# DeltaNet and maxout on one core: the first chunk's inverse by doubling on TensorE, and pairs of chunks shifted by one

## The chip, the cores and the metric

The kernel runs on one core of a Trainium2 chip. The metric is the device time of one execution, in microseconds (us). All profiles quoted are in the fast state. Each run of a changed kernel stood beside runs of the kernel before on the same chip. A ratio is the mean time of one kernel's fast runs over the mean of the other's of the same rounds, so it isn't quite the ratio of the medians that are quoted. A span is the length of the one profiled execution.

Engines: PE is TensorE, DVE is VectorE, ACT is ScalarE, POOL is GpSimd, SP is SyncE, which here only issues transfers.

## The reference

```python
# q, k, v: (4, 8, 768, 48), beta: (4, 8, 768), all float32
k_n = k / (norm(k) + 1e-6)
for t in range(S):
    y[:, :, t] = q[:, :, t] @ state
    v_old = k_n[:, :, t] @ state
    state = state + beta[t] * outer(k_n[:, :, t], v[:, :, t] - v_old)
x = y.transpose(0, 2, 1, 3).reshape(3072, 384)
h = maximum(maximum(x @ w1, x @ w2), x @ w3)      # three 384 x 768 matrices
return h @ w_out                                   # 768 x 384
```

The recurrence is computed in 12 chunks of 64 steps. Within a chunk it needs the inverse of a unit triangular 64x64 matrix for each batch and head. Between chunks only a state is handed on.

## The kernel before

Two chunks make a group of 512 tokens; there are six groups. For each chunk TensorE forms Gram products of the keys (`p_g`). Two chunks at a time, VectorE inverts the four 32x32 diagonal blocks of each head by forward substitution, 31 steps of two operations, with one matrix on each of 128 partitions:

```python
def solve(m):                      # m: pair of chunks (2m, 2m+1)
    ...                            # norms and beta: ten small operations
    for j in range(BL - 1):        # BL = 32
        nc.vector.tensor_tensor(out=t_v, in0=x[:, j, ...], in1=y[:, 0:a, j, ...], op=ALU.mult)
        nc.vector.tensor_tensor(out=y[...], in0=y[...], in1=t_v, op=ALU.subtract)
        yield                      # another part of the program is placed here
    ...                            # to DRAM as y_d and x_d, back as ut2, t1 and ut: SP's queue
```

TensorE then joins the blocks (`p_z`, `p_j`), takes the state into account (`p_k`, `p_q`), solves (`p_u`), moves the state on (`p_s`), forms the output (`p_y`) and transposes it (`p_x`) into `xt`. These are the *small products*: a chunk's `p_u`, for instance, has 64 of 64x48. The maxout part of a group follows:

```python
def ffn(m):
    for f in range(6):
        for i in range(3):                       # a maxout step: p_h
            ...                                  # three products, 128 x 128 by 512 columns
            # i == 0: ACT copies p_h to h; else DVE takes max(h, p_h)
    for i in range(4):
        ...                                      # p_o: six products of 384 columns
```

The weights come as 24 pieces, each fetched into one of four buffers (`w_bits`) and converted by three operations on VectorE (`mant`), two on GpSimd (`mant`, `w_sb`) and one on ScalarE (`up`). All transfers that matter are issued in order on SP's queue: fetches of pieces, loads of keys and queries, and the solve's results. The opening is in program order. Behind it a scheduler orders each engine's instructions by its own estimate of when they are ready; that order is fixed when the program is built.

The solve of a group's pair of chunks runs about one group ahead of its use:

```python
for m in range(GROUPS):
    for i, _ in enumerate(ffn(m)):
        ...
        if i == SOLVE:                  # 12 of 22 steps
            solving = solve(m + 2)      # z of that group: step 3 of the next group
        if i >= SOLVE:
            some(solving, 4)
        links(m + 1, LINKS.get(i, ""))  # small products of the next group, spread
```

## Time and profile before

| | before |
|---|---|
| median of 4 runs (lowest, highest) | 621.76 us (621.56, 623.07) |
| span of the profiled run | 622.2 us |
| TensorE busy, idle | 544.3, 77.9 us |
| VectorE busy | 317.6 us |
| first maxout product | 74.4 us |
| second half of group 0 starts | 143.8 us |

The prediction shows the strips, the stretches by group and the chain. Three more stretches will be compared later. Each line has: stretch, length, busy time (and instructions) of PE, of its weight loads, of DVE, ACT and POOL, then the granted PE clock, the DMA share and GB/s.

```profile
0.00:74.40 74.40, 34.65 (x743) 27.79 (x743) 41.63 (x109) 26.68 (x44) 23.60 (x49) 0.66 0.77 156
74.40:143.80 69.40, 48.49 (x962) 38.67 (x963) 57.78 (x143) 17.34 (x34) 23.72 (x27) 0.92 0.43 102
...
143.80:622.20 478.40, 461.18 (x6014) 258.49 (x6014) 218.16 (x498) 109.47 (x177) 39.97 (x47) 0.99 0.31 62
```

At 143.8 us half of group 0's maxout products are done: in this kernel these are the first three of the six blocks `f`, of both chunks (the `p_x` of chunk 1 came at 98.0 us).

### The profile page before, as it was taken

What the parts mean: (1) busy time and instruction counts of PE and PEld (TensorE: products, weight loads), DVE (VectorE), ACT (ScalarE), POOL (GpSimd) and SP (SyncE); (2) the same over time, 40 slices, a digit from 0 to 9 for tenths busy, and PEclk for the clock granted to TensorE, in tenths of its full rate; (3) what the DMA queues carried; (4) which work ended last, traced back from release to release, by engine and by line L of the source; (5) the groups of instructions that cost most, each with busy time, mean ns of one, the idle gap of its engine ahead of it and who ended that gap; (6) DMA issues with size and microseconds to landing.
All of it is one profiled execution on the core that took longest, in us unless ns stands there. A gap on an engine that the chain in (4) does not pass through costs nothing.

```text
span 622.2 us, 17590 instructions
## 1 busy us (share of the span) xinstructions
PE 544.3 (87%) x7718; PEld 324.9 (52%) x7718; DVE 317.6 (51%) x748; ACT 153.5 (25%) x255; POOL 87.3 (14%) x123
## 2 busy tenths in 40 slices
PE   5361786676799999999999999999999999999997
PEld 4251675452555554655655545555555555554444
DVE  0797159998364982369722499132596222101110
ACT  4333222323421232221332121432112120110001
POOL 7102204445141002000110000200000100000000
PEclk9656599887799999999999999999999999999999
DMA  9775813553771544352355321542103400020002
GB/s 196 141 162 123 184 34 110 137 112 72 205 124 20 108 99 91 79 95 52 77 111 98 65 52 27 106 91 44 36 1 79 77 2 3 3 49 1 0 0 51
DMA packets 158412, 48.47 MB, mean 78 GB/s; under 512 B 143296, under 2 KB 153344, under 8 KB 158336
## 3 DMA queue, kind: packets, MB, share of 16 engines
q1 hardware_dynamic: 156096, 46.87, 36.3%
q8 instruction: 60, 0.98, 0.7%
q10 hardware_dynamic: 2112, 0.39, 0.4%
q14 instruction: 16, 0.13, 0.1%
q0 software_dynamic: 128, 0.10, 0.1%
HBM read 31.56 MB, written 15.73 MB: 76 GB/s over the span
## 4 chain that ended last, share of the span: by engine, by line
PE 66%; DVE 23%; issue 4%; ACT 2%; DMA 2%; POOL 1%; SPq 0%; POOLq 0%; ACTq 0%; DVEq 0%
PE p_h L591 39%; PE p_o L615 11%; DVE tmp L376 7%; DVE y_bl L382 7%; PE p_t L285 3%; PE p_g L307 3%; PE p_u L516 2%; PE p_s L534 2%; PE p_k L488 2%; PE p_y L551 1%; PE p_q L488 1%; PE p_z L447 1%; DVE h L601 1%; PE p_j L466 1%; DVE mant L208 1%
## 5 line engine op out<-in xcount | busy, mean ns | idle before, releaser
L591 PE MATMUL p_h<-xt,w_sb 128*128 128x512 f32 (+1 forms) x702 | 301.4, 578 | 18.8 <-POOL w_sb L216 7.2
L591 PEld LDWEIGHTS p_h<-xt,w_sb 128*128 128x128 f32 x702 | 131.3, 195 | 145.6 <-issue 117.2
L601 DVE TENSOR_TENSOR h<-h,p_h 128x512 f32<-128x512 f32 (+1 forms) x78 | 50.2, 644 | 148.5 <-PE p_h L591 147.3
L615 PE MATMUL p_o<-wo_sb,h 128*128 128x384 f32 x288 | 96.5, 489 | 1.6 <-DVE h L601 1.5
L615 PEld LDWEIGHTS p_o<-wo_sb,h 128*128 128x128 f32 x288 | 53.6, 190 | 39.7 <-DVE h L601 4.6
L376 DVE TENSOR_TENSOR tmp<-x_bl,y_bl 128x31 f32<-128x31 f32 (+15 forms) x186 | 69.2, 372 | 4.9
L382 DVE TENSOR_TENSOR y_bl<-y_bl,tmp 128x31 f32<-128x31 f32 (+15 forms) x186 | 65.8, 354 | 4.6
L599 ACT COPY h<-p_h 128x512 f32<-128x512 f32 (+1 forms) x39 | 21.6, 553 | 129.7 <-PE p_h L591 129.7
L258 POOL TENSOR_TENSOR v_t<-v_t,nrm 128x768 f32<-128x768 f32 x12 | 17.8, 1482 | 175.1 <-DMA v_t<-in_v_dram 51.1
L307 PE MATMUL p_g<-kqt 64*64 64x64 f32 (+1 forms) x1280 | 33.4, 250 | 8.4 <-ACT kqt L291 7.1
L307 PEld LDWEIGHTS p_g<-kqt 64*64 64x64 f32 x1280 | 28.3, 149 | 16.8 <-ACT kqt L291 10.0
L291 ACT COPY kqt<-p_t 128x1024 f32<-128x1024 f32 (+1 forms) x28 | 24.6, 890 | 28.6 <-PE p_t L285 28.5
L285 PE MATMUL p_t<-ident,kpad 128*128 128x128 f32 x96 | 19.1, 333 | 11.5 <-DMA kpad<-in_k_dram 11.5
L623 ACT COPY o_sb<-p_o 128x384 f32<-128x384 f32 x24 | 11.5, 479 | 67.6 <-PE p_o L615 64.5
L203 POOL TENSOR_SCALAR mant<-mant 128x384 f32<-128x384 f32 x24 | 14.4, 600 | 82.7 <-DVE mant L199 57.7
L540 DVE TENSOR_TENSOR st<-st,p_s 128x768 f32<-128x768 f32 x11 | 10.5, 951 | 28.3 <-PE p_s L534 28.3
L456 POOL COPY ut<-ut 32x512 f32<-32x512 f32 x24 | 14.6, 608 | 72.9 <-DMA ut<-y_d 71.9
L285 PE MATMUL p_t<-ident,qpad 128*128 128x128 f32 x96 | 17.7, 313 | 7.1 <-DMA qpad<-in_q_dram 5.2
L447 PE MATMUL p_z<-ut,at 64*32 64x32 f32 x768 | 10.8, 203 | 14.8 <-DMA ut<-y_d 14.8
L317 DVE TENSOR_TENSOR pt<-p_g,mask 128x512 f32<-128x512 f32 x24 | 16.4, 687 | 11.2 <-PE p_g L307 11.1
L216 POOL TENSOR_TENSOR w_sb<-mant,up 128x384 int32<-128x384 int32 x18 | 18.8, 1045 | 23.9 <-DVE mant L212 12.7
L325 ACT COPY at<-p_g 128x512 f32<-128x512 f32 x24 | 14.0, 585 | 32.1 <-DVE pt L317 26.6
(74 smaller groups left out, 444.6 us busy)
## 6 DMA issues: line engine op xcount, KB each, us to landing
w_bits<-in_moe_w_dram SPq DMA_DIRECT2D x18, 384.0 KB, 4.3
at_d<-at SPq DMA_DIRECT2D x48, 128.0 KB, 3.2
qpad<-in_q_dram SPq DMA_DIRECT2D x48, 96.0 KB, 3.4
v_t<-in_v_dram SPq DMA_DIRECT2D x24, 192.0 KB, 4.3
out_dram<-o_sb SPq DMA_DIRECT2D x48, 96.0 KB, 2.2
kpad<-in_k_dram SPq DMA_DIRECT2D x44, 96.0 KB, 3.1
x_bl<-at_d SPq DMA_DIRECT2D x24, 128.0 KB, 3.1
y_d<-y_bl SPq DMA_DIRECT2D x12, 256.0 KB, 3.5
```

The source lines that it names most:

```text
L216: nc.gpsimd.tensor_tensor(out=dst.bitcast(I32), in0=mant_v.bitcast(I32), in1=up_v, op=ALU.add)
L258: nc.gpsimd.tensor_tensor(out=vts[c], in0=vts[c], in1=nrm[:, :, :, None].to_broadcast([128, 2, H, D]), op=ALU.mult,)
L285: nc.tensor.transpose(p_t[:, i, j * 128 : (j + 1) * 128], src[:, 2 * j : 2 * j + 2], ident,)
L291: nc.scalar.copy(kqt.rearrange("p j b i t -> p i (j b) t")[:, some], p_t.rearrange("p i (x t) -> p i x t", t=C)[:, some],)
L307: nc.tensor.matmul(p_g[rows(bb ^ (g * i)), par, c0 : c0 + C * (1 + whole)], kq[:, 0], kq if whole else kq[:, i],)
L376: nc.vector.tensor_tensor(out=t_v, in0=x[:, j, None, j + 1 :].to_broadcast([128, a, b]), in1=y[:, 0:a, j, None].to_broadcast([128, a, b]), ...
L382: nc.vector.tensor_tensor(out=y[:, 0:a, j + 1 :], in0=y[:, 0:a, j + 1 :], in1=t_v, op=ALU.subtract,)
L488: nc.tensor.matmul(p_b[rows(bb), par, c0 : c0 + D], kqt[g][rows(par), j, bb ^ g, i], st[rows(par), bb ^ g, g, j],)
L591: nc.tensor.matmul(p_h, w_sb[i][:, t, f * 128 : (f + 1) * 128], xt[:, t, lo : lo + w], start=(t == 0), stop=(t == KT - 1),)
L599: nc.scalar.copy(h, p_h)
L601: nc.vector.tensor_tensor(out=h, in0=h, in1=p_h, op=ALU.max)
L615: nc.tensor.matmul(p_o, hs[f][:, i * 128 : (i + 1) * 128], wo_sb[:, f], start=(f == 0), stop=(f == FT - 1),)
```

## The change

The intent is to start maxout long before the first solve on VectorE could be finished. Chunk 0 is solved on TensorE by doubling: blocks of 1, 2, 4 ... 32 are combined in six levels of small products. The forward substitution takes the other chunks in pairs shifted by one, (1,2), (3,4) ... (11). Groups 0 and 1 go through maxout in halves of 256 columns, one chunk each, so that chunk 0 need not wait for chunk 1. The core of the diff, with cuts:

```diff
+    class First:                                  # chunk 0
+        def step(self, lv, part):                 # one of six levels, half of the heads
+            ...  # p_a: 16 products of 64x64 (not in the last level)
+            ...  # p_r: 16 products of 64x112 (64x48 in the last two)
+            ...  # DVE masks p_a into zt, ACT copies p_r into ar
...
-    early = FT // 2 if m == 0 else 0              # only half of group 0's p_h in halves
-    for lo in (0, TOK // 2):
-        for f in range(early):
-            yield from hidden(f, lo, TOK // 2)
+    parts = 2 if m < 2 else 1
+    w = TOK // parts
+    for i in range(parts):
+        for f in range(FT):
+            yield from hidden(f, i * w, w)
+        for j in range(4 // parts):
+            yield from result(i * (4 // parts) + j)
...
-            nc.vector.tensor_scalar(               # a weight piece
-                out=mant_v, in0=high, scalar1=0x7FFFFFFF, scalar2=None,
-                op0=ALU.bitwise_and,
-            )
+            nc.scalar.activation(
+                out=mant_v.bitcast(FP32), in_=high.bitcast(FP32),
+                func=mybir.ActivationFunctionType.Abs,
+            )                                      # and joined one piece later
...
-                solving = solve(m + 2)             # begun at step 12, used in the next group
+    for p in range(4, PAIRS + 1):                  # the pair of chunks (2p-1, 2p)
+        m = p - 2
+        at_end = 37 if m == 2 else 18
+        SOLVES[p] = ((m - 1, at_end), (m - 1, at_end + 2), (m, 7))
+        # plan of group m: z of that pair at step 10, chunk 2p-1 ready (x) at step 18
```

The Gram products of keys and queries, one product of 128 columns for half of the units before, are two of 64 columns now. The opening, up to the end of chunk 0, is in program order.

## The prediction

> **What bounds the kernel now.** I read the page's strips first, then the chain that ended last, then busy time by stretches, then single instructions.
>
> ```profile
> PE   5361786676799999999999999999999999999997
> DVE  0797159998364982369722499132596222101110
> PEclk9656599887799999999999999999999999999999
> ```
>
> Each character is 15.6 us. TensorE (PE) is full from the twelfth slice to the end at full clock. The loss lies in the first eleven, where VectorE (DVE) has its nines. The chain says the same: PE carries 66%, DVE 23%.
>
> ```profile
> 0.00:74.00 74.00, 34.25 (x738) 27.48 (x742) 41.63 (x109) 26.53 (x44) 23.60 (x49) 0.66 0.77 155
> 74.00:223.00 149.00, 120.76 (x2126) 82.58 (x2119) 108.73 (x258) 41.41 (x77) 42.23 (x49) 0.92 0.48 108
> 302.00:391.00 89.00, 86.92 (x1291) 49.70 (x1289) 50.22 (x122) 24.32 (x37) 6.33 (x7) 1.00 0.37 73
> 391.00:478.00 87.00, 85.80 (x1288) 49.59 (x1288) 43.62 (x98) 20.79 (x32) 4.86 (x6) 1.00 0.26 54
> ```
>
> The columns are stretch, length, busy time of PE, weight loads, DVE, ACT and POOL, PE clock, DMA share, GB/s. The first stretch ends where maxout begins; in it the inverses of the first two chunks are solved on DVE. The second is the first group of maxout (149 us); the last two are ordinary groups (89 and 87 us) with PE over 97% busy. So about 74 + 60 us at the start are in play, nothing after.
>
> ```profile
> 556.14 46.35 PE p_h L591 x108
> 602.49 15.49 PE p_o L615 x48
> 228.77 3.00 DMA y_d<-y_bl
> 231.82 1.97 DMA ut<-y_d
> ```
>
> These chain lines (start, length, what) give the last group, maxout alone: 46.35 + 15.49 = 61.8 us. The lower two are the hand-over after a solve: 5.2 us from the last DVE operation to p_z.
>
> **What the Trainium skill says.** "FP8 and Floating Point Precision", TensorE Precision Notes, gives true FP32 four passes through the array. With the 2.4 GHz of "TensorE: Matmul & The Clock Gate", a 512-column product is an estimated 4 x 512 / 2.4 = 853 ns; the trace has 46.35 / 54 = 858 ns (two recorded instructions per product). So late PE time cannot shrink. "TensorEngine Tiling (Array Packing)", Key Properties, says tiles work independently. The trace agrees: 64 recorded 64x48 instructions of p_k add 1.08 us to the chain, 17 ns each, though one is listed at 220 ns. That makes the new inverse on PE cheap. "SBUF — State Buffer", "SBUF: two separate sides", calls the port that DVE and GpSimd share an exclusive lock. The trace agrees: the same 135-element operation takes 0.30 us alone and 1.09 us beside a weight addition of POOL.
>
> ```profile
> 31.15 0.30 DVE L376 TENSOR_TENSOR tmp<-x_bl,y_bl 128x135 f32<-128x135 f32 x1
> 101.51 1.09 DVE L376 TENSOR_TENSOR tmp<-x_bl,y_bl 128x135 f32<-128x135 f32 x1
> 101.30 1.14 POOL L216 TENSOR_TENSOR w_sb<-mant,up 128x384 int32<-128x384 int32 x1 [0.77 <-DVE mant L212]
> ```
>
> **The change, part by part.** The built program's order on each engine shows where things stand, without times.
>
> *The first chunk.* Before, maxout waits for the first solve (DVE 28.7 to 52.4 us, 31 steps of two operations), two DMA hops, p_z, p_j, p_u, p_y and p_x. Now chunk 0 needs keys, norms, one transposition and six doubling levels on PE. My sum: keys land at 6.3 us as before; 16 warm-up instructions and cold transpositions leave kqt at about 8.5; level masks (21 small DVE operations, 0.17 us each) delay the two norm sums (0.55 each) to 8; ten small DVE/ACT operations of 0.2 to 0.25 give the factors at 11.7; four 512-element key operations (0.65) end at 14.3. They hold two of three PSUM pairs, so other keys' products wait; transposed blocks are masked by about 18.5, and two units are turned by 19.5. A level is two halves, each with 32 recorded 64x64 instructions (17 ns: 0.54 us) and 32 of 64x112 (four passes in four tiles: 0.75 us). PE needs 2.6 us, ACT two copies of 896 (about 0.93 each, from 0.80 for 768), DVE four masks of 256 (0.41). With latency and inserted transpositions and weight pieces I take 3.3, 3.3, 4.2, 4.2, 3 and 2: 20 us. Then u, p_y, y, p_x, xt in halves, 4.5 us. Maxout starts at about 44 instead of 74.4 us.
>
> *The pairs shifted by one chunk.* Chunks (1,2), (3,4) ... (11) still make six solves. DVE loses no solve. Off its path come 24 `mant` operations of 0.51 us (12 us, now on ACT). It gains about 15 us of masks and keys in the opening.
>
> *Chunk by chunk.* The first half of group 0 (18 products of 256 columns, two outputs) can run while DVE solves (1,2). It waits for that solve and the weights. Before, a solve with 13 pieces filled DVE from 93.3 to about 146 us. Of those 53 us the new order removes 13 x 0.35 (at least) for `mant`, four masks (0.6), three maxima (0.33) and a subtraction (0.9), some 9, and adds three sums of norms (1.5) and the small prelude (about 2.2). So the solve lasts 46 to 48 us: 44 to 91. PE, needing some 34 us there, idles. Behind it DVE has seven pieces left; with the POOL operations (0.60 + 1.05 us) that is 12 to 14 us, since POOL sets the pace. The order puts both outputs before the next p_z: the last piece leaves another 4.5 us of p_o. Then p_z 0.7, z copies 1.3, p_j 1, ut 1.3, p_u 1.1, u 0.8, p_y 1.1, y 0.95, p_x 0.7, xt 0.8: 10 us. The second half starts at 91 + 13 + 4.5 + 10 = 118 us.
>
> *The rest at PE's rate.* Maxout left: 162 products of 256 columns at 0.435 us (18 recorded ones took 4.17 us, at most 0.46 per product with fill), 216 of 512 at 0.86, 22 outputs at 3.87: 70.5 + 185.8 + 85.1 = 341. Small work, counted from the order: ten p_k (1.08), p_q (0.93), p_u (1.08), p_y (1.0) and p_x (0.68), nine p_s (1.08), p_z and p_j (0.97), 28 groups of four transpositions (0.44), and 17 double gram products (1.0): 104. Gram products in pairs of 64 columns, instead of 128 at once, add 0.1 us per chunk, included. With 2.5% for bubbles (89 and 87 us against 61.8 + 23.4 = 85.2 of such work) it is 456. The solve hand-overs of (3,4) and (5,6) are nearly even with PE's work. For (3,4), DVE has a prelude of 3.5 us, 62 operations interleaved at about 0.32 (20), a copy 1, 22 maxima of 0.35 (7.7), four updates of 0.87 (3.5), six norm sums of 0.46 (2.8) and 3 of masks and norms: 41, plus 5 of hand-over. PE has until that p_z 23 steps of three products (30), two outputs (7.7) and some 10 of small work: 48. For (5,6) I count 42 + 5 against 44. I give 5 us for both. The last output's copy and DMA: 3 us.
>
> Sum: 118 + 456 + 5 + 3 = **582 us**, 6.4% shorter. Calibration on the kernel before: at 143.8 us it had an estimated 454 us of PE work and took 478, so 24 us of stalls. My 19 us after 118 (11 + 5 + 3) is lower because the order has room for DMA.
>
> **Rivals.**
> 1. *The new opening is slow.* A chain of PE, DVE and ACT with short bursts could run at half clock: "TensorE: Matmul & The Clock Gate", Part 1, says idleness returns the gate to half rate, and the trace shows 0.50 for 52 to 74 us, when PE was busy 9.3 of 22 us. PE is fuller in the new levels, which speaks against it. If it came, levels cost 5 to 6 us: maxout at 56, time 594.
> 2. *DVE and POOL simply become the bound in the first group.* Starting maxout 30 us earlier does not finish (1,2) 30 us earlier if pieces, locks and solve pile up; I have charged most of this. If each of the 24 pieces costs one full lock of 0.8 us extra, 12 to 15 us more: about 596. If instead moving Abs to ACT unties DVE from POOL, the hand-over shrinks by 10: about 570.
> 3. *Input transfers.* DMA was 77% busy to 74 us (155 GB/s). By 44 us the new opening wants about 7.6 MB (eight key and four query units of 192 KB, two v of 384, four products of 256, blocks 0.5 MB: 4.6; eight weight pieces of 384 KB: 3), 49 us at that rate. Weights are last, so pieces come late rather than keys; this could add 5 to 8 us, but the first half was waiting anyway.
> 4. *Hidden anyway.* If the solve of (3,4) took the place of the first, the early start would be lost: about 605. Against it, its 41 us lie beside 48 us of PE work.
>
> **Range and chances.** Rivals 1 and 2 each reach up by 12 to 15, the favourable side of 2 down by 12; PE's remaining work is known to some 6 us. So 564 to 602. Faster by over 2% means below 609.5 us, which needs both adverse rivals: 0.96 faster, 0.035 the same, 0.005 slower.
>
> **What would show it.** The first p_h at 40 to 48 us; levels about 20 us long at a clock near 0.9; the solve of (1,2) ending at 86 to 96 us with DVE over 90% busy; p_h after chunk 1's xt at 112 to 124; then PE over 96% busy to the end, ordinary groups still 85 to 89 us, the last group 62. It is wrong if maxout starts after 55 us, if PE has long gaps after 125 us, or if the group steps became longer.

## More of the kernel before

What PE waited for shows in the view of waits (what waited, for whom: us in total, times, longest).

```profile
PE p_z L447 <- DMA ut<-y_d: 14.8, 4, 8.5
...
PE p_h L591 <- DVE h L601: 5.4, 4, 2.5
```

The first product after a solve waits for its results (9.0 of the 14.8 us in the opening). PE waits for a maximum of VectorE only 5.4 us in all.

## The result, and the profile after

| | before | after |
|---|---|---|
| median (lowest, highest), 4 runs each | 621.76 (621.56, 623.07) | 648.38 (645.65, 650.37) us |
| ratio, 95% interval | | 1.0421 (1.0379 to 1.0462) |
| span of the profiled run | 622.2 | 648.4 us |
| TensorE busy, idle | 544.3, 77.9 | 571.7, 76.7 us |
| first maxout product | 74.4 | 55.3 us |
| second half of group 0 starts | 143.8 | 145.0 us |

The changed kernel is 4.2% slower. The prediction of 582 us was 66 us too low, far outside its range. The totals already say something odd: TensorE does 27.4 us more and idles just as long as before. The strips of the page after (16.2 us a character):

```profile
PE   6866787779797999796989988999899999999997
...
DVE  6357998435972379522398131695323963201110
...
PEclk7986687979998999899998989999999999999999
```

PE is better filled in the first four slices than before. But its sixes, sevens and eights go on to the middle of the kernel, where the strip before had only nines. The stretches, to set beside the three above:

```profile
0.00:55.30 55.30, 39.60 (x1147) 35.50 (x1147) 27.58 (x75) 24.40 (x43) 23.08 (x49) 0.82 0.81 151
55.30:145.00 89.70, 66.83 (x1019) 50.93 (x1019) 65.79 (x149) 39.60 (x79) 36.10 (x45) 0.83 0.58 133
...
145.00:648.40 503.40, 465.31 (x6569) 294.00 (x6568) 235.36 (x571) 106.15 (x178) 28.43 (x31) 0.98 0.28 54
```

Maxout starts 19 us sooner, but the first half and what follows it take 89.7 us, and at 145.0 us TensorE has 465.3 us of work left. The kernel before had 461.2 left at 143.8 us. So there is no lead left by then. (At both marks as much of `p_h` is left; the kernel before has two more of the 24 outputs to do.) Behind it after takes 25.0 us more: 4.1 of work and 20.9 of idle time (38.1 against 17.2). Half clock is in that work: where the view of windows has a granted clock of 0.50, TensorE is busy for 19.5 us of this stretch after and 12.0 before, which makes some 3.7 us of the difference. The chain's end is as it was: the lengths of the last group's two parts are the same to 0.01 us.

```profile
581.99 46.35 PE p_h L808 x108
628.34 15.49 PE p_o L825 x48
```

What PE waited for, after:

```profile
PE p_h L808 <- DVE h L818: 16.1, 10, 3.7
PE p_g L370 <- issue: 7.1, 5, 2.2
...
PE p_j L678 <- issue: 5.7, 4, 1.9
...
PE p_z L659 <- DMA ut<-y_d: 0.5, 1, 0.5
```

The waits for solves are nearly gone. In their place PE waits for maxima, and for nothing that the profile shows ("issue"). Adding up all such lines from 145.0 us on, I get 15.6 us of issue and 12.9 of maxima after; in the stretch from 143.8 us before they were 2.9 and 1.7. Three lines from the timeline of PE after show the first (start, length, instruction, in brackets the gap before it and what ended it):

```profile
296.61 1.09 PE L370 MATMUL p_g<-kqt 64*64 64x64 f32 x58 [1.60 <-issue]
...
301.44 0.37 PE L744 MATMUL p_s<-u,kpad 64*64 64x48 f32 x10 [0.89 <-issue]
...
305.71 0.39 PE L370 MATMUL p_g<-kqt 64*64 64x64 f32 x10 [2.18 <-issue]
```

From 290 to 306.7 us the small products of a chunk stand in one run, without a product of maxout between them. The gaps cut through groups (10 of 64 are left after the last one). In another such run, from 372 us, they come at multiples of 128 recorded products, each with its weight load. The second kind, on PE and then on DVE:

```profile
341.19 4.42 PE L808 MATMUL p_h<-xt,w_sb 128*128 128x512 f32 x6 [3.16 <-DVE h L818]
```

```profile
338.17 1.58 DVE L587 TENSOR_TENSOR tmp<-x_bl,y_bl 128x256 f32<-128x256 f32 x1
339.67 0.54 DVE L309 TENSOR_REDUCE ksum<-ksq 128x8 f32<-128x384 f32 x1
...
340.47 0.67 DVE L818 TENSOR_TENSOR h<-h,p_h 128x512 f32<-128x512 f32 x1
```

The maximum that PE waits for stands behind steps of a solve in VectorE's fixed order, one of them lengthened from 0.42 to 1.58 us beside a GpSimd operation at 337.9 us. After the gap six recorded products take 4.42 us instead of the 2.6 of the last group; from 342.3 to 345.7 us the granted clock is 0.50.

Between these there is the hand-over of the first solve. It ends on VectorE at 105.67 us. SP's queue, after:

```profile
115.56 0.33 SPq L232 DMA_DIRECT2D w_bits<-in_moe_w_out_dram  x1
115.99 1.15 SPq L601 DMA_DIRECT2D y_d<-y_bl  x2
```

The result leaves 10.3 us late, behind fetches of weight pieces that wait for a free buffer. The last piece is done at 125.8 us; only then can the first half's `p_o` end, and `p_z` comes at 127.4. PE, after:

```profile
125.87 1.56 PE L825 MATMUL p_o<-wo_sb,h 128*128 128x384 f32 x4 [0.43 <-POOL wo_sb L278]
127.36 1.16 PE L659 MATMUL p_z<-ut,at 64*32 64x32 f32 x68
```

### The profile page after: what moved, and what is told of

It reads as the page before. It is cut to its first block, busy times and chain, and to the rows that moved or that the text cites. A ratio compares the mean times of both kernels' runs of the same rounds, so it can differ in the third digit from the quotient of the medians.

```text
span 648.4 us, 19709 instructions
## 1 busy us (share of the span) xinstructions
PE 571.7 (88%) x8733; PEld 380.4 (59%) x8733; DVE 328.7 (51%) x794; ACT 170.1 (26%) x300; POOL 87.6 (14%) x124
## 4 chain that ended last, share of the span: by engine, by line
PE 62%; DVE 26%; issue 7%; ACT 2%; POOL 2%; DMA 1%; SPq 0%; POOLq 0%; ACTq 0%; DVEq 0%
PE p_h L808 31%; PE p_o L825 12%; DVE tmp L587 8%; DVE y_bl L593 7%; PE p_g L370 3%; PE p_t L348 3%; PE p_r L542 2%; DVE h L818 2%; PE p_k L700 2%; PE p_u L726 1%; PE p_q L700 1%; DVE mant L274 1%; PE p_z L659 1%; PE p_j L678 1%; PE p_y L761 1%
## 5 line engine op out<-in xcount | busy, mean ns | idle before, releaser
L808 PE MATMUL p_h<-xt,w_sb 128*128 128x256 f32 (+1 forms) x864 | 307.5, 507 | 29.2 <-DVE h L818 16.1
L808 PEld LDWEIGHTS p_h<-xt,w_sb 128*128 128x128 f32 x864 | 164.2, 197 | 138.2 <-issue 90.2
L818 DVE TENSOR_TENSOR h<-h,p_h 128x256 f32<-128x256 f32 (+1 forms) x96 | 52.8, 550 | 135.4 <-PE p_h L808 135.3
L816 ACT COPY h<-p_h 128x256 f32<-128x256 f32 (+1 forms) x48 | 22.9, 478 | 142.2 <-PE p_h L808 142.1
L370 PE MATMUL p_g<-kqt 64*64 64x64 f32 x1536 | 34.8, 238 | 10.3 <-issue 7.1
L370 PEld LDWEIGHTS p_g<-kqt 64*64 64x64 f32 x1536 | 30.4, 150 | 14.7 <-issue 10.1
L833 ACT COPY o_sb<-p_o 128x384 f32<-128x384 f32 x24 | 11.5, 479 | 93.5 <-PE p_o L825 85.8
L354 ACT COPY kqt<-p_t 128x512 f32<-128x512 f32 (+1 forms) x34 | 25.3, 760 | 24.2 <-PE p_t L348 24.1
L278 POOL TENSOR_TENSOR w_sb<-mant,up 128x384 int32<-128x384 int32 x18 | 18.0, 1001 | 18.4 <-DVE mant L274 11.4
L665 DVE COPY z<-p_z 32x512 f32<-32x512 f32 x11 | 7.6, 689 | 21.6 <-ACT z L664 21.6
L542 PE MATMUL p_r<-ar,zt 64*64 64x112 f32 (+1 forms) x384 | 13.6, 267 | 5.6 <-issue 2.8
L308 ACT ACTIVATE ksq<-kpad 128x384 f32<-128x384 f32 x22 | 11.5, 523 | 26.1 <-DVE ksum L309 16.3
L761 PE MATMUL p_y<-u,pt 64*64 64x48 f32 x768 | 15.7, 231 | 2.6 <-issue 2.6
```

Of the source, the lines that this page charges most:

```text
L354: nc.scalar.copy(kqt.rearrange("p j b i t -> p i (j b) t")[:, some], p_t.rearrange("p i (x t) -> p i x t", t=C)[:, some],)
L370: nc.tensor.matmul(p_g[rows(bb ^ (g * i)), par, j * C : (j + 1) * C], kqt[rows(par), j, bb ^ g, 0], kqt[rows(par), j, bb ^ g, i],)
L542: nc.tensor.matmul(p_r[rows(to(bb, g)), g, i * w : (i + 1) * w], zt[g][r, hs.start + i], self.ar_v[r, g, hs.start + i, c0:],)
L761: nc.tensor.matmul(p_v[rows(bb), g, h], pt[g][rows(bb ^ g), h], u[rows(bb ^ g), g, h])
L808: nc.tensor.matmul(p_h, w_sb[i][:, t, f * 128 : (f + 1) * 128], xt[:, t, lo : lo + w], start=(t == 0), stop=(t == KT - 1),)
L816: nc.scalar.copy(h, p_h)
```

## The experiments

Seventeen kernels ran, three rounds each. One run of no_wo and one of order_all counted as slow, being over 1.5% above the fastest of their kernel; the ratios leave them out. "Second half" is the start of the maxout products of chunk 1 in the profiled run of a changed kernel, "rest" is from there to the end of the span. In these rounds the kernel before had medians of 623.7 to 624.4 us, some 2 us above the 621.76 of the first. So a gain that is read from medians against 648.38 comes out some 2 us small; the ratios do not have this fault.

| run | median us | ratio to before (95%) | span | first p_h | second half | rest |
|---|---|---|---|---|---|---|
| after | 648.38 | 1.042 (1.038, 1.046) | 648.4 | 55.3 | 145.0 | 503.4 |
| start_late | 649.33 | 1.039 (1.037, 1.042) | 646.7 | 66.7 | 144.6 | 502.1 |
| levels_bare | 660.77 | 1.059 | 659.9 | 56.1 | 156.5 | 503.4 |
| solve_early | 661.07 | 1.061 (1.055, 1.067) | 665.1 | 67.2 | 155.0 | 510.1 |
| solve_early_q | 659.45 | 1.057 (1.051, 1.063) | 656.3 | 70.2 | 150.7 | 505.6 |
| no_wo | 644.65 | 1.030 (1.021, 1.039) | 640.9 | 52.5 | 137.5 | 503.4 |
| no_weights_after | 624.89 | 1.001 (0.997, 1.005) | 622.1 | 54.0 | 118.5 | 503.6 |
| no_weights_before | 607.14 | 0.972 (0.968, 0.976) | 605.6 | 72.7 | | |
| abs_alone | 627.26 | 1.004 (1.001, 1.007) | 624.7 | 76.7 | | |
| burst_dense | 650.82 | 1.043 (1.041, 1.046) | 648.0 | | | |
| burst_spread | 645.14 | 1.034 (1.031, 1.037) | 643.7 | | | |
| order_all | 712.44 | 1.142 | 707.5 | 55.0 | 159.5 | 548.0 |
| order_pe | 655.17 | 1.050 (1.046, 1.054) | 653.4 | 54.5 | 150.8 | 502.6 |
| solve_half_after | 637.73 | 1.022 (1.018, 1.026) | 634.1 | 55.8 | 144.4 | 489.7 |
| solve_half_before | 629.37 | 1.008 (1.005, 1.012) | 626.9 | | | |
| solves_sooner | 642.22 | 1.029 (1.026, 1.032) | 639.3 | 56.7 | 145.8 | 493.5 |
| sooner_all | 648.15 | 1.037 (1.033, 1.040) | 646.4 | 55.8 | 147.1 | 499.3 |
| sooner_pe2 | 657.01 | 1.050 (1.043, 1.057) | 653.1 | 55.8 | 147.2 | 505.9 |

### Where the early start went

**start_late**: dummy work before the first maxout product.

```diff
+    p_d = ps_ffn([128, TOK], "p_d")
+    for _ in range(16):
+        nc.tensor.matmul(p_d[:, 0 : LEVELS * C], ident, level.rearrange("p l c -> p (l c)"))
     opening.close()
```

> The kernel after with some 10 us of dummy products (16 of 384 columns, 0.64 us each at full clock) put on TensorE between the opening and the first maxout product. If the earlier start of maxout is hidden behind the solve of (1,2) and the weights, the time moves by less than 3 us (646 to 651); if what is gained at the start is gained at the end, it grows by about 10 (658).

Maxout started 11.4 us later, and the second half at the same time. PE's timeline:

```profile
66.72 1.46 PE L808 MATMUL p_h<-xt,w_sb 128*128 128x256 f32 x6
...
144.64 2.86 PE L808 MATMUL p_h<-xt,w_sb 128*128 128x256 f32 x12
```

The time did not change (ratio 1.039 against 1.042). More than half of the 19 us by which maxout starts sooner is worth nothing.

**no_weights_after** and **no_weights_before**: both kernels without any conversion of weights; the results are wrong.

```diff
+    pieces = []
     staged = deque()
...
-    conv = weights()
+    conv = iter(())       # and the four weight matrices set to zero on GpSimd
```

> The kernel after without any conversion of weights: all four matrices are zero (a wrong result on purpose); 24 pieces less on VectorE (0.9 us each), GpSimd (1.5) and ScalarE (1.1), and no fetch that holds up the queue. Theory 'the pieces beside the solve hide the early start': the second half, at 145 us in after, starts at 112 to 122, and the time falls by 20 to 32 us (to 616 to 628), the rest of the loss lying behind 145 us. Rival: the solve alone holds it; the second half starts after 130 and the time is over 634.

> The kernel before without any conversion of weights, in the same way. If the pieces hide the early start in the kernel after alone, this one gains less than that one: 10 to 20 us (602 to 612), so the gap of 26 us between the two kernels shrinks to 10 to 20. Rival: both gain alike and the gap stays at 26 us or grows.

In the first, the solve's result left at 86.2 us (116.0 in after), and the second half started where the theory put it. The second had its expected gain too. PE's timeline, then the windows of both kernels from 118.5 us on, the changed one first:

```profile
118.50 2.86 PE L809 MATMUL p_h<-xt,w_sb 128*128 128x256 f32 x12
```

```profile
118.50:622.10 503.60, 467.34 (x6574) 296.85 (x6568) 235.19 (x571) 106.03 (x178) 28.54 (x31) 0.97 0.28 55
118.50:605.60 487.10, 465.18 (x6037) 261.26 (x6036) 212.32 (x492) 107.37 (x171) 29.40 (x33) 0.99 0.28 56
```

So the pieces and their fetches beside the solve hold back the second half by 26.5 us, and the time fell by 23.5 (medians; 25.8 by the ratios). How much of it is conversion and how much the fetches in SP's queue was not separated. The rest stayed at 503.6 us. What follows the second half takes the same 502 to 504 us in after, start_late, levels_bare, no_wo and here (505.6 and 510.1 in the two solve_early kernels). The kernel before gained 17.2 us by its medians, so the gap shrank to 17.8. But even without pieces the change has no lead: at 118.5 us PE had 467.3 us of work left in the changed kernel and 465.2 in the kernel before. The early start fills idle time of the opening, and the new products on PE (`p_r` 13.6, `p_a` 10.5 and the warm-up 3.4: 27.5 us) use it up.

**no_wo**: after, without the six pieces of the last matrix.

```diff
-    for t in range(FT):
-        pieces.append((wo_sb[:, t : t + 1], bits[:, t : t + 1], (1, DM)))
+    zeros(wo_sb)          # wrong result on purpose
```

> The kernel after without the conversion of the six pieces of the last weight matrix, which is zero instead (a wrong result on purpose): six pieces less on VectorE (0.9 us each), GpSimd (1.5) and ScalarE (1.1), which stand between the end of the first solve at 105.7 us and the first half's p_o. If those pieces, and the hand-over stuck behind their fetches on the queue, hold the second half, it starts 8 to 15 us sooner and the time is 634 to 641; if the solve alone does, it moves by less than 4 us.

The second half came 7.5 us sooner, just below what was expected. The median fell by only 3.7 us, but by the ratios the gain is 1.3%, some 8 us, as in the profile. The runs spread from 638 to 648, so the time itself decides little. The rest was again 503.4 us.

**abs_alone**: the kernel before with the new form of the weight pieces alone (the third hunk of the diff above).

> The kernel before with the weights part of the change alone: the bit masking of each piece by Abs on ScalarE instead of VectorE, joined one piece later. 24 x 0.51 us leave VectorE, some 12 of them in the first group, where VectorE is the bound: theory 5 to 10 us shorter (612 to 617). Rival: ScalarE's Abs and the piece of lag make the pieces later, so 0 to 3 us longer.

The theory failed: 0.4% slower, although it took 24 `mant` operations off VectorE. The rival (0 to 3 us longer, as the pieces come later) fits. VectorE's busy time fell by 4.9 us only, from 317.6 to 312.7, though those operations had taken 12.3. So this part of the change alone gains nothing; whether the relief of VectorE is worth something that later pieces take back was not tested.

**levels_bare**: six pieces moved out of the levels, behind chunk 0's `xt`.

```diff
         if lv in (2, 3):
             gram_q(lv - 2)
             load_q(lv + 1)
-            some(conv, 1)          # likewise at three other places before to_x(0)
...
     to_x(0)
+    some(conv, 1)
+    for _ in range(5):
+        some(conv, 1)
+        fetch()
     solving = solve(1)
```

> The changed kernel with the six weight pieces of the opening moved from inside the doubling levels to behind xt of chunk 0. Theory O (pieces on ACT and DVE inside the levels stretch the opening from 44 to 55 us): xt of chunk 0 comes 5 to 8 us earlier, the first p_h perhaps not, since the pieces are then late; time within 5 us of 648, as the first half waits for the solve and the weights anyway. If the opening's length were what lost the gain, the time would fall by 5 us or more. If neither xt moves, the levels are bound by their own chain or by the fetch.

The opening hardly became shorter: `p_x` of chunk 0 came at 50.9 instead of 52.5 us. The second half came 11.5 us later, and the time was 12 us longer, which neither expectation had. So the pieces inside the levels make up 1.6 us of the slow opening. Behind it they came late: the last was done at 134.4 us instead of 125.8.

**solve_early**: the first 15 steps of the first solve inside the opening, where VectorE is idle half the time. (The expectation counts 18; the edit moves three at each of five places.)

```diff
         first.step(lv, 1)
+        if lv == 3:
+            solving = solve(1)
+            some(solving, 1)
+        # and three steps at each of five later places of the opening
```

> The kernel after, with the prelude and 18 of the 31 steps of the first solve (chunks 1 and 2) put between the doubling levels 3 to 5 and p_x, where VectorE is idle about half the time; the levels may grow by up to 8 us. Theory 'the first half is hidden behind VectorE's solve and pieces': maxout starts up to 8 us later, but chunk 1's xt and the second half come 6 to 12 us sooner (at 133 to 139 instead of 145) and the time falls to 636 to 643. Rival: the weight pieces alone set the second half, so it moves by less than 3 us (over 645).

This miss taught most. The solve ended on VectorE at 97.8 instead of 105.7 us, little for 15 of 31 steps, and its result left at 103.0 instead of 116.0. But the last weight piece was done at 141.5 instead of 125.8 us. The first maxout product came 12 us later; PE now waited 5.2 us for VectorE's copy of `u` and 4.1 us for that of `xt`. Then PE lost what was left:

```profile
125.25 1.09 PE L348 MATMUL p_t<-ident,qpad 128*128 128x128 f32 x4 [10.95 <-DMA qpad<-in_q_dram]
```

The load of these queries had been issued at 120.3 us, behind the solve's reads on SP's queue.

**solve_early_q**: the same, with query loads from ACT's queue.

```diff
-    def load_q(n, queues=one_queue):
+    def load_q(n, queues=(nc.scalar, nc.scalar)):
```

> The kernel solve_early with the query loads issued from ScalarE's queue instead of SyncE's. In solve_early TensorE stood 10.9 us before a transposition whose queries' load was issued only at 120 us, behind the solve's reads on SyncE's queue, and the time was 661. If that queue is what turned the sooner solve (ended 103 us) into a loss, the wait goes, the second half starts 8 to 14 us sooner (141 to 147 instead of 155) and the time is 645 to 654. Rival: the weight pieces come just as late and the time stays over 656.

The wait was gone, but the rival was right: the second half came only 4.3 us sooner. (The 103 us of the expectation is when the result left, not the end of the solve.) The last weight piece was now done at 147 us instead of 125.8, and PE waited for the pieces of `wo_sb`. Solve and pieces share VectorE and GpSimd: moving one forward moved the other back.

### Dense runs of small products

**burst_dense** and **burst_spread**: the kernel before with 1024 extra products of 64x64 in its last group, in one run or in 16 blocks of 64 between maxout steps.

```diff
     for i, _ in enumerate(ffn(m)):
+        if m == GROUPS - 1 and i < 16:
+            for _ in range(16 if i == 3 else 0):     # spread: range(1)
+                block()                              # 64 recorded products
```

> The kernel before with 512 extra FP32 products of 64x64 (1024 recorded instruction pairs) in one run between the fourth and fifth p_h step of the last group, where nothing but maxout is left. Results are not used. Theory F (TensorE's instructions are fetched in blocks of 128 pairs, one block per about 3.5 us as the strip of DMA in the dense stretch of the changed kernel shows, so dense small products starve): the burst takes about 8 x 3.5 = 28 us, minus what is buffered, with gaps of 1 to 2 us put down to issue after each 128 pairs; time about +24 to +28 us. Rival (the issue gaps come from PSUM buffers or semaphores of the real chain, not from fetching): 17 ns a pair, 17.4 us, no gaps; time +17 us.

> The same 512 extra products, but 32 after each of sixteen p_h steps of the last group. Theory F: each block of 64 pairs (1.1 us) stands between steps of 2.58 us, so the fetch is ahead: +17 us, no issue gaps over 0.5 us. Rival: the same +17 us as the dense one; theory F wants the dense one 7 to 11 us slower than this one, the rival wants them equal within 2 us.

PE's timeline in burst_dense, and from its view of DMA (556 to 600 us) the queue that fetches instructions (transfers, MB, share):

```profile
566.97 4.17 PE L731 MATMUL p_b<-ident 64*64 64x64 f32 x266
571.96 2.10 PE L731 MATMUL p_b<-ident 64*64 64x64 f32 x128 [0.81 <-issue]
575.69 2.10 PE L731 MATMUL p_b<-ident 64*64 64x64 f32 x128 [1.64 <-issue]
579.45 2.10 PE L731 MATMUL p_b<-ident 64*64 64x64 f32 x128 [1.66 <-issue]
```

```profile
q8 instruction: 9, 0.15, 1.4%
```

After 266 products a gap comes every 128, and the period settles at 3.5 to 3.8 us for 2.10 us of work. The spread blocks took 1.16 us each and had no such gaps. The dense kernel was 26.7 us slower than before, as theory F had it; the spread one 21.1 instead of 17, since a step with its block took 3.87 us, where a step alone takes 2.58. So the difference is 5.7 us: less than the 7 to 11 of theory F, more than the 2 of the rival. The Trainium skill, "Runtime: NRT & Kernel Launch", Instruction fetch mechanics, says that instructions are refilled in blocks of 16 KiB, 256 instructions, and that crossing a boundary is mostly hidden. 128 products with their weight loads are 256 instructions, so the position of the gaps agrees. The packets kept in the trace settle it: each transfer of that queue is of 16,384 bytes (in after it made 68, room for 17,408 instructions, and PE ran 17,466 products and weight loads); each of the six gaps in the burst ended 1.2 to 1.4 us after one had landed, and the next one began about 1.1 us after that. That the refill is hidden does not hold here for dense small products. The "issue" gaps of the changed kernel are the same: the four from 290 to 306.7 us end 1.4 to 1.6 us after such a block has landed.

### The solves' lead

In the kernel before a solve's result was sent off 53 to 68 us before the `p_x` of the first chunk that needed it (groups 2 to 5). In after this is 33 to 47 us from chunk 3 on. Since the pairs are shifted by one, a solve serves the second chunk of the group that comes next and the first of the one behind. The theory "half the lead" was that this lateness shows up as dense runs, because the scheduler can place the small products only behind the solve.

**order_all** and **order_pe**: all engines, or PE alone, in program order to the end, where the small products are spread.

```diff
-    opening.close()
     tc.no_sync_barrier()
...
                 do(name)
+    opening.close()          # order_pe: the order of PE alone is kept
```

> The changed kernel with all engines kept in program order to the end (no scheduler after the opening): small products then stand between p_h steps and the two outputs of chunk 0 come after p_z and p_j of chunk 1, solve operations come two or three per step. Theory F (dense stretches and the order they stand in cost the time after 145 us): waits of TensorE put down to issue fall from 23 us to under 9, waits for h on DVE from 16 to under 8, time 600 to 625. Rival D (the solve on DVE is the bound in every group whatever the order): waits move to p_z waiting for the DMA of ut, or stay at h; time within 10 us of 648.

> The kernel after with TensorE alone kept in program order to the end (the other engines as the scheduler puts them). The small products then stand spread between maxout steps instead of in runs of up to 368 instructions, but p_z stands earlier than its solve may have ended. Theory 'fetch and cold clock in the dense runs cost some 20 us': waits put down to issue fall from 23 us to under 10, and if the solves keep up, the time falls to 630 to 640. Rival 'the solves are late': the time goes into waits of p_z and of the maxima instead, and is 650 or more, as when all engines were kept in program order (712).

With all engines in program order it was far worse than either expectation (712 us; `p_z` waited for the solve's transfers 40.3 us, `p_h` for maxima 31.8). With PE alone, waits are instructive:

```profile
PE p_z L659 <- DMA ut<-y_d: 21.0, 11, 5.1
PE p_h L808 <- DVE h L818: 16.4, 13, 2.3
```

In the rest after the second half, issue fell from 15.6 to 1.4 us, and waits of `p_z` rose from 0.5 to 14.3: named waits of 32.9 us in all, against 33.2 in after. The rival was right. As the solves end now, these two orders of PE give either the dense runs or the waits, at the same price.

**solve_half_after** and **solve_half_before**: every second step left out of all solves but the first (wrong).

```diff
-        for j in range(BL - 1):
+        for j in range(0, BL - 1, 2 if m > 1 else 1):     # before: m > 0
```

> The kernel after, with every second step left out of each forward substitution except the first one (a wrong result on purpose; 16 of 31 steps stay, some 10 us of VectorE fewer per solve, from the pair (3,4) on). Theory 'half the lead': since the pairs are shifted by one chunk, each solve is needed half a group earlier than before, so its end sets when the small products of a chunk can be placed, and they bunch up behind it. Then the time falls by 15 to 30 us against after (to 618 to 633), and the waits of TensorE for the maxima fall from 16 us to under 9. Rival 'TensorE itself': the loss after the first group comes from the added small products and the fetch of their instructions, whatever the solve does; then it falls by less than 6 us (over 642).

> The same cut in the kernel before, for every solve but the first (a wrong result on purpose). Theory 'half the lead': from its second group on the kernel before had a whole group of slack between a solve and its use, so only the solve of chunks 2 and 3 beside the weights can gain: 0 to 10 us (612 to 622), nothing after 223 us. Rival: if solves are exposed in both kernels alike, it falls by 15 us or more.

After gained 10.7 us by its medians (12.5 by the ratios), which lies between the two theories. All of it lies in the rest, 489.7 instead of 503.4 us:

```profile
144.30:634.10 489.80, 462.71 (x6577) 293.02 (x6568) 186.45 (x421) 105.84 (x178) 28.64 (x31) 0.98 0.29 56
```

PE idles there for 27.1 instead of 38.1 us. The waits for maxima fell less than expected, from 16.1 to 13.7. Before did not gain at all; it became 0.8% slower. Its instruction order on all engines was built anew as well, so some 5 us may be what a new order does by chance; one run cannot tell. The two kernels differ by more than that: VectorE's time for the later solves counts in the changed kernel, and in the kernel before no cost of it shows.

**solves_sooner**, **sooner_all** and **sooner_pe2**: the later solves begun sooner; the same for the first two groups as well; PE besides in program order from the third group on, with `p_z` one step later.

```diff
-        SOLVES[p] = ((m - 1, at_end), (m - 1, at_end + 2), (m, 7))
+        SOLVES[p] = ((m - 1, at_end - 1), (m - 1, at_end), (m, 5))
# and in the plan of a group: Gram products at steps 9 and 14 instead of 15
# sooner_all: three instead of two solve steps per step in groups 0 and 1; SOLVES[3] at (1, 7)
# sooner_pe2: manual order of PE from m == 2 on; z at step 11 instead of 10
```

> The kernel after, with the gram products, blocks and solves from the pair (7,8) on placed one to six units earlier in the plans (a unit is one maxout step). By the built order the run of small products of the last two shifted groups is broken up (from 368 and 192 instructions to pieces under 130), that of the others stays. Theory 'half the lead' with bunching: 4 to 8 us shorter than after (640 to 644). Rival: no change within 2 us.

> The kernel solves_sooner with the solves of the first two groups hastened too: three steps instead of two for each maxout step of 256 columns, and the solve of chunks 5 and 6 begun one or two steps sooner. By the built order the dense runs of these groups stay as they are (274, 302 and 278 instructions). If only the order counts, no change against solves_sooner (640 to 644); if the solve's own end counts, 3 to 6 us shorter.

> The kernel solves_sooner with, besides, TensorE in program order from the third group on and the small products one step later in the plan, so that they stand spread and p_z stands about where the sooner solve ends. Theory 'late solves force a choice between dense runs and waits of p_z': with the solve sooner both shrink, so it beats solves_sooner by 3 to 8 us (634 to 639). Rival: p_z or the maxima wait instead and it is no better than solves_sooner (642 or more).

The first won 6.2 us as expected (8.2 by the ratios), in the profile all of it behind the second group; issue in the rest was 10.6 instead of 15.6. The second gave that back, against both of its expectations. It did not wait longer: in the rest PE idled for 30.4 us (31.8 in solves_sooner), but was busy for 469.0 instead of 461.7, of which 27.2 instead of 12.7 us fell in stretches that the clock records have at 0.50. The third became slower than after, as its rival had it, with new waits of `p_z` and of `p_h` for ACT. Set against some 5 us of chance, solves_sooner supports the theory but doesn't carry it alone.

No kernel tried that computes the right result beats the kernel before.

## Why the prediction was wrong

The gap of 66 us is the sum of two: the second half started at 145.0 instead of 118 (27 us), and what follows took 503.4 instead of 464 us (39 us). By the prediction's own steps:

1. **"Maxout starts at about 44"**: 55.3. The levels took about 29 us instead of 20. Its rival 1 was half right: the clock granted in the opening was 0.82, and 0.50 from 45.3 us on; gaps put down to issue took 4.5 us of the levels. The weight pieces between them took only 1.6 (levels_bare). Since start_late shows that 11 us here cost nothing, this step was wrong without consequence for the time.
2. **"the solve lasts 46 to 48 us"** was nearly right: 50.4 us, from 55.3 to 105.7, with VectorE busy for 47.95 of it.
3. **"Behind it DVE has seven pieces left ... 12 to 14 us"**, with 4.5 for `p_o` and 10 for `p_z` to `xt`: the mechanism was right and the size off. The pieces ended 20.1 us after the solve, and from `p_z` at 127.4 to the second half took another 17.6 us instead of 10, with two issue gaps of 2.4 us and 6.8 us at half clock in it. Rival 2 named 12 to 15 us more here; the sum left them out. The test without pieces gave 118.5 us, but with a solve whose result left at 86; that it meets the predicted number is partly chance.
4. **"The rest at PE's rate"**, 341 + 104 = 445 us of work: 465.3. The term mis-sized most is the rate of maxout. It was taken from the last group, where nothing stands between the products and the clock is full (858 ns). The records of neighbours overlap, so time that they share is counted once here. Then 216 products of 512 columns took 193.4 us (895 ns) and 162 of 256 took 76.1 (470 ns): 269.5 instead of 256.3 us. The outputs took 85.7 instead of 85.1, the small products 110.2 instead of 104. About half of these 20 us is half clock (19.5 us of busy time fell in it), which the prediction allowed for in the opening alone. The kernel before showed 896 ns in the same place (266.2 us for 297), and the calibration could have found it: it estimated 454 us of PE work and 24 of stalls from 143.8 us on, where the windows have 461.2 and 17.2. "Gram products in pairs of 64 columns ... add 0.1 us per chunk" was too low too: 22.7 us for eight and a half chunks after, 16.0 for seven before, so 0.4.
5. **"That makes the new inverse on PE cheap"**: 27.5 us of PE work was added, more than the 19 us by which maxout starts sooner. The opening was judged by when it ends, not by the work left. Time plus work left is 55.3 + 532.1 = 587.4 us in after and 74.4 + 509.7 = 584.1 before (work left is all busy time less that of the first stretch). So the early start on these terms is no lead. With the prediction's own figures the sum would still have shown one: behind the start of maxout it counted 34 us of the first half, a hand-over and 445 us, where TensorE then had 66.8 and 465.3 us of work.
6. **"The solve hand-overs of (3,4) and (5,6) are nearly even with PE's work"**, at 5 us for both: with the bubbles (2.5%, although its own 88 against 85.2 us are 3.3%) and the last output, 19 us of idle time were allowed, and 38.1 came. Rival 4 (a later solve takes the place of the first) was nearest to what happened, at 605 us. It was looked for as a wait of `p_z`, of which there is 0.5 us. It came in another form: the order built around late solves puts the small products in dense runs, which fetch slowly, and maxima behind solve steps. This part is shown by order_pe (the waits change form at the same sum) and by solve_half_after (13.7 us of the 25 come back).
7. What was to show it wrong did: maxout after 55 us, long gaps after 125 us, and the ordinary stretches from 346 to 440 us idle for 8 of 94 us.

What stays open: about 11 us of the rest stay when the solves are halved (489.7 against 478.4 before). Issue (11.9) and maxima (10.3) are still its waits then, but no run removed them both, so it isn't shown whether the other half of the solves or something else holds them. Whether a longer lead could be had was not tried beyond one or two steps: the eight key and six transposed buffers set where the Gram products can stand.

## What to carry to other kernels

Compare two plans by the bounding engine's time plus all of its work left at the same point, not by when that engine starts its main work: a head start bought with work on the same engine is none. When a dependence is moved to the middle of a group, look at how long the slack of every later producer becomes; if it falls short, the loss may not appear as a wait for that producer, but as a bunched order, slow fetch and waits elsewhere. Take the rate of an operation from a stretch with the same neighbours.

## What the Trainium skill lacked or had wrong

- "Runtime: NRT & Kernel Launch", Instruction fetch mechanics, calls the crossing of a 16 KiB boundary mostly hidden. In dense runs of 64x64 products with their weight loads each 256 instructions took 3.5 to 3.8 us for 2.10 us of work, with gaps of 1.4 to 1.7 us; only the first 266 products came without a gap.
- "TensorEngine Tiling (Array Packing)", Key Properties, says that a change of the tiling mode drains TensorE, and gives no size. An FP32 product of 512 columns by 128 rows took 858 ns among its like and 895 among small products of other tilings (some 885 without the half-clock stretches). In burst_spread a step with a block of 64 small products took 3.87 us, where the step alone takes 2.58 and half of a dense run of 128 about 1.05. Whether a drain is what costs this was not tested.
